# A gated linear attention kernel with two projections after it: tiles of q, k and exponentials laid out by chunk, guard reductions held behind layer two's slots

## Chip, core and metric

The kernel runs on one core of one Trainium2 chip. The metric is the device time of one execution in microseconds, the median of several runs. Engines are named as the profile names them: PE (TensorE), DVE (VectorE), ACT (ScalarE), POOL (GpSimd) and SP (SyncE, here only a queue that issues DMAs).

## Reference

4 batches of 8 heads, 768 steps, head size 48. A complex decay per step and channel, its magnitude clipped to 0.999, acts on a 48 x 48 state; then come two dense layers over 3072 tokens.

```python
mag = np.sqrt(a_re * a_re + a_im * a_im)
scale = np.minimum(mag, 0.999) / (mag + 1e-06)
a_re_n, a_im_n = (a_re * scale, a_im * scale)
for t in range(S):
    new_re = ar * S_re - ai * S_im
    new_im = ar * S_im + ai * S_re
    S_re, S_im = (new_re + kv, new_im)          # kv = outer(k[t], v[t])
    y[:, :, t] = np.einsum('bhd,bhde->bhe', q[:, :, t], S_re)
# layer one (384 -> 2048 -> 384), layer two the same with another gate
h = x @ w_in; g = h * np.clip(h + 3.0, 0.0, 6.0) / 6.0;         x = g @ w_out
h = x @ w_in; g = h * (1.0 / (1.0 + np.exp(-1.702 * h)));       out = g @ w_out
```

## The kernel before

Only the function `chunked_path` runs its work here; `general_path` behind it is taken when a flag says that the inputs left the range that the fast path assumes. The flag comes from guards: small reductions on DVE whose results `check_range` gathers.

**Preparation** (`prep_ops`). The 3072 tokens form 12 blocks of 256 tokens, each of two chunks of 128. For one block, 384 feature rows lie as three groups j of 128 partitions. ACT and DVE turn the decay into running products E and rotations cos and sin, and multiply q and k by them. The tiles `qk` and `E` (named `pE` in the profile) have the shape [128, q or k, (j, chunk), 129]: 128 steps, and one column more for the last decay. Block 0 is prepared chunk by chunk, the others whole.

**Repacking** (`repack`, L478 to L487). Attention wants heads on 96 partitions, so DMAs copy from `E` and `qk` into the tile `QK` ([96, 16, 129]; 48 partitions from `E`, 48 from `qk`). A chunk takes 12 DMAs: per source two of 48 partitions and 6 x 129 words, and four small ones for the rows that the three groups have left over. They alternate between the queues of SP and POOL, in block 0 between SP, POOL and ACT. Two buffers of `QK` exist (tag QK); the raw weights of layer two and the guards' loads use the same two.

**Attention** (`att_ops`). Per chunk PE makes scores (`sc`, L518), DVE masks them (`p`, L522), PE turns k (`kt`) and adds up the outputs (`yps`) and the state (`ud`). `slot(q, h)` says which of the 16 slots of `QK` holds a head's q or k.

**Layers.** One slot is an input projection (`h`, L635, nine matmuls), a gate in four steps on ACT and DVE (`gate1` to `gate4`; `gh` L655, `gl` L660) and an output projection (`o`, L673) that follows two slots later. A layer has 16 slots for each block of 512 tokens, six such blocks; at the end of a block ACT copies three accumulators out (`y`, L677) before PE can start the next block's output projections.

**Order.** For the first 82 slots of layer one, the text `PLAN` fixes the order on DVE, ACT and PE by hand. SP's and POOL's queues, and everything after the plan, are ordered by the compiler's planner, which places an instruction where its own estimate of time finds it ready.

**Guards.** After the plan `wdecode` loads, checks (`check_w`, L374) and decodes layer two's weights, 16 loads of 768 KB. In layer two `recheck_w` loads layer one's 16 weight tiles again and checks them, `recheck_a` loads four tiles of `a`, then `check_range` follows; the program hands them to the planner behind the slots `end[last + FT + 8 + i * 3]`; `last` is the first slot of layer one's last block, so `last + FT` is layer two's slot 0, and the guards stand at its slots 8, 11, 14 and so on to 68.

Of the kernel before, what the change touches and what calls it, by code (L numbers as in the profile page):

```python
# [9 lines left out]
F32 = mybir.dt.float32  # L10
# [4 lines left out]
AF = mybir.ActivationFunctionType  # L15
ALU = mybir.AluOpType
# [241 lines left out]
def chunked_path(ctx: ExitStack, tc, flag, a_t, qk_t, v_t, w1i, w1o, w2i, w2o, out):  # L258
# [34 lines left out]
    def stat_col(k, n=1):  # L293
        n_used[k] += n
        return stat[k][:, n_used[k] - n:n_used[k]]
# [44 lines left out]
    raw, w32, marks, wparts = {}, {}, {}, {}  # L340

    def load_w(m, kind, j):
        src = ((w1i, w1o), (w2i, w2o))[m][kind]
        t = at2.tile([P, 768, 2], U32, tag="QK", name="ws")
        nc.sync.dma_start(out=t.rearrange("p n w -> p (n w)"), in_=src[j].bitcast(U32))
        return t

    def recheck_w(i):
        check_w(load_w(0, i % 2, i // 2))

    def recheck_a(p):
        t = at2.tile([P, 768], F32, tag="QK", name="as")
        nc.sync.dma_start(out=t, in_=a_t[p, :, 0:3 * TB])
        V.tensor_reduce(out=stat_col("re"), in_=t, axis=mybir.AxisListType.X, op=ALU.min)

    def load_first(i):
        kind, j = i % 2, i // 2
# [13 lines left out]
        split_lo(V, 0, i % 2, i // 2, w32.pop(i))  # L371

    def check_w(t):
        V.tensor_reduce(out=stat_col("w"), in_=t.bitcast(F32)[:, :, 1], axis=mybir.AxisListType.X, op=ALU.min, apply_absolute_value=True)  # L374

    def split_hi(m, kind, j, x):
        w = wp.tile([P, 2, 768], F32R, tag=f"w{'io'[kind]}{j}", name=f"w{'io'[kind]}{j}")
# [14 lines left out]
    def load_in(b, parts="aq", c=None):  # L392
        if "a" in parts:
            if (b, "a") not in ins:
                ins[b, "a"] = prep.tile([P, 2, 3, TB], F32, tag="a", name="a")
            o, n = (0, TB) if c is None else (c * CH, CH)
            nc.sync.dma_start(out=ins[b, "a"].rearrange("p q j t -> p (q j) t")[:, :, o:o + n],
                              in_=a_t[b].rearrange("p (q j t) -> p (q j) t", q=2, j=3)[:, :, o:o + n])
        if "q" in parts:
            if (b, "qk") not in ins:  # L400
                ins[b, "qk"] = prep.tile([P, 2, 6, CE], F32, tag="qk", name="qk")
            qk = ins[b, "qk"]
            if c is None:
                nc.sync.dma_start(out=qk[:, :, :, 0:CH], in_=qk_t[b].rearrange("p (q c t) -> p q c t", q=2, t=CH))
            else:
                nc.sync.dma_start(out=qk.rearrange("p q (j c) t -> p (q j) c t", c=2)[:, :, c, 0:CH],
                                  in_=qk_t[b].rearrange("p (q j t) -> p (q j) t", q=2, t=TB)[:, :, c * CH:c * CH + CH])

    v_c = {}

# [4 lines left out]
    def prep_ops(b, c0, nch):  # L415
# [1 line left out]
        ts = c0 * CH  # L417
        ops = {}
        op = ops.__setitem__
        both = lambda t: t.rearrange("p q (j c) t -> p q j c t", c=2)[:, :, :, c0, 0:CH] if nch == 1 else t[:, :, :, 0:CH]  # L420
        bothc = lambda t: t.rearrange("p (j t) -> p j t", t=CH).unsqueeze(1).to_broadcast([P, 2, 3 * nch, CH])

        def tmp(nm):
            if (b, nm) not in ins:
                ins[b, nm] = prep.tile([P, 2, 6, CE] if nm == "E" else [P, 3 * TB], F32, tag=nm if nm == "E" else "p" + nm, name="p" + nm)
# [7 lines left out]
        sel = lambda t, q: t[:, q].rearrange("p (j c) t -> p j c t", c=2)[:, :, c0:c0 + nch, 0:CH]  # L433
        selc = lambda t: t.rearrange("p (j c t) -> p j c t", j=3, c=nch)
        col = lambda t, i: t.rearrange("p q (j c) t -> p q j c t", c=2)[:, :, :, c0:c0 + nch, i]
# [29 lines left out]
        op("turns", lambda: V.tensor_scalar(out=pB(), in0=pB(), scalar1=MAGIC, scalar2=None, op0=ALU.subtract))  # L465
        op("frac", lambda: V.scalar_tensor_tensor(out=pA(), in0=pA(), scalar=2.0 / TURN, in1=pB(), op0=ALU.mult, op1=ALU.subtract))
        op("keep", lambda: V.tensor_scalar(out=carry, in0=r3(pA())[:, :, n - 1:n], scalar1=0.5 * TURN, scalar2=0.0, op0=ALU.mult, op1=ALU.add))
        op("sin", lambda: tact(pC(), pA(), AF.Sin, scale=TURN))
        op("abs", lambda: act(pB(), pA(), AF.Abs))
        op("cos", lambda: tact(pB(), pB(), AF.Sin, scale=-TURN, bias=bhp))  # L470
        op("qkE", lambda: V.tensor_tensor(out=both(qk()), in0=both(qk()), in1=both(E()), op=ALU.mult))
        for d, t in (("qk", qk), ("E", E)):
            op("last" + d, lambda t=t: tact(col(t(), CH), selc(pC())[:, :, :, CH - 1].unsqueeze(1).to_broadcast([P, 2, 3, nch]), AF.Exp, scale=0.5))
        op("qkcos", lambda: V.tensor_tensor(out=both(E()), in0=both(qk()), in1=bothc(pB()), op=ALU.mult))  # L474
        op("qksin", lambda: V.tensor_tensor(out=both(qk()), in0=both(qk()), in1=bothc(pC()), op=ALU.mult))

        def repack(c, y, queues):
            if 2 * b + c not in qk_c:  # L478
                qk_c[2 * b + c] = at2.tile([96, 16, CE], F32, tag="QK", name="QK")
            t = qk_c[2 * b + c][48 * y:48 * y + 48]  # L480
            z = ins[b, "E" if y == 0 else "qk"].rearrange("p q (j c) t -> p q j c t", c=2)[:, :, :, c, :]
            parts = [(t[:, 6 * g:6 * g + 6, :], z[48 * g:48 * g + 48].rearrange("p q j t -> p (q j) t")) for g in range(2)]
            parts += [(t[d0:d0 + nr, 2 * h:2 * h + 2, :], z[r0:r0 + nr, :, j, :]) for r0, nr, j, h, d0 in ((96, 32, 0, 6, 0), (96, 16, 1, 6, 32), (112, 16, 1, 7, 0), (96, 32, 2, 7, 16))]
            for i, (dst, src) in enumerate(parts):
                e = (nc.sync, nc.gpsimd, nc.scalar)[i % (3 if b == 0 else 2)]
                if e in queues:
                    e.dma_start(out=dst, in_=src)  # L487
# [8 lines left out]
    xs = {}  # L496

    def slot(q, h):
        return (h % 2) * 6 + q * 3 + h // 2 if h < 6 else 2 * h + q

    def att_ops(c):
        b = c // 2
# [68 lines left out]

        def um():
            u = ud4() if first else u4
            g = qk_c[c][:, 0:12, CH:CE].rearrange("p (r q i) c -> p q i r c", r=2, q=2)[:, 1].to_broadcast([96, 3, 2, D])
# [41 lines left out]
    ht, gt, ops_ = {}, {}, {}  # L616
    slots = []
    for m in range(2):
        for b in range(NT // TK):
# [37 lines left out]

    def gate4(s):
        lo = gp.tile([P, s[3], s[5]], F32R, tag="gl", name="gl")
        V.tensor_tensor(out=lo, in0=gt[s][0], in1=gt[s][1], op=ALU.subtract)  # L660
        gt[s].append(lo)

    def outproj(s):
# [47 lines left out]
    def wload(n=1):  # L711
        for _ in range(n):
            if n_loaded[0] < len(wseq):
                raw[n_loaded[0]] = load_w(*wseq[n_loaded[0]])
                n_loaded[0] += 1

    def wdecode(x):
        i = n_decoded[0]
        check_w(raw[i])
        decode_weight(V, raw.pop(i), x)  # L720
        w32[i] = x
        n_decoded[0] += 1
        wload()
# [55 lines left out]
    with tc.manual_schedule(engines={mybir.EngineType.DVE, mybir.EngineType.Activation, mybir.EngineType.PE}):  # L779
        for token in PLAN.split():  # L780
            planned(token)

    end = {i: [] for i in range(len(slots))}
    last = slots.index((0, NT // TK - 1, 0, 1, 0, TK))
    wload(2)
    for k in range(2 * NPR):
        at = N_PLAN + k * (FT + 8) // (2 * NPR)
        end[at].append(lambda k=k: wdecode(spare(k)))
        end[max(at, last + k // 2 * 2 + 2 + k % 2 * LAG)].append(wsplit)
    at, n = last + 2 * FT, len(slots) - last - 3 * FT  # L790
    late = [lambda i=i: recheck_w(i) for i in range(2 * NPR)] + [lambda p=p: recheck_a(p) for p in range(LATE)] + [check_range]
    for i, f in enumerate(late):
        end[last + FT + 8 + i * 3].append(f)
    for c in range(NT // CH):
        end[slots.index((1, c * CH // TK, 0, 1, 0, TK)) - FT + 4 + 2 * (c % (TK // CH))].append(lambda c=c: load_x2(c))
    for i in range(N_PLAN, len(slots)):
# [59 lines left out]
```

## Time and profile before

| | us |
|---|---|
| median of three runs | 1019.45 (1017.28 to 1020.99) |
| the profiled execution | 1014.48 |
| its span, first to last instruction | 1012.8 |
| PE busy in it | 953.2 |
| DVE busy | 643.1 |
| ACT busy | 519.7 |

The profile is one execution. Times in it run from the start of the span. A line such as L518 is the line of the kernel. In a wait, the name behind the arrow is what ended last before the waiting instruction could start. PEclk is the granted share of TensorE's clock: 1.00 is the level of 2.4 GHz, 0.50 that of 1.2 GHz.

### The profile page before, as it was taken

How to read it: one execution, taken by the hardware profiler on the slowest of the kernel's cores; microseconds unless marked ns; L12 is line 12 of the kernel's file. 1: busy time of each engine (PE TensorE's matmuls, PEld its weight loads, DVE VectorE, ACT ScalarE, POOL GpSimd, SP SyncE). 2: the span in 40 equal slices, each digit the busy share in tenths (PEclk: the TensorE clock that was granted, in tenths of full speed). 3: DMA queues.
4: the chain of work that ended last, by engine and by line, in shares of the span. 5: the costliest groups of instructions: out<-in, count | busy, mean ns of one | idle time of the engine just before them, and what ended most of it. 6: DMA issues, size and time to landing. Idle time of an engine off the chain costs nothing.

```text
span 1012.8 us, 14367 instructions
## 1 busy us (share of the span) xinstructions
PE 953.2 (94%) x5378; PEld 802.7 (79%) x5378; DVE 643.1 (63%) x919; ACT 519.7 (51%) x862; POOL 111.8 (11%) x218
## 2 busy tenths in 40 slices
PE   1479999999999999999999999989999999999997
PEld 1378988898788888887788888768888888888885
DVE  6789998885866777577549998573343433433332
ACT  5767677675765786566426554233243333433322
POOL 2110212213303123030310000000000000000000
PEclk9779999999999999999999999999999999999999
DMA  8873425354535254233325447670020010100001
GB/s 307 246 234 79 127 63 111 97 122 111 117 90 139 64 126 117 56 96 94 71 83 191 138 151 224 238 233 21 1 63 1 24 40 1 47 1 1 32 1 34
DMA packets 82524, 101.04 MB, mean 100 GB/s; under 512 B 9104, under 2 KB 71824, under 8 KB 82448
## 3 DMA queue, kind: packets, MB, share of 16 engines
q1 hardware_dynamic: 73872, 88.44, 29.4%
q0 software_dynamic: 7936, 11.36, 5.0%
q8 instruction: 44, 0.72, 0.3%
q10 hardware_dynamic: 640, 0.26, 0.1%
q14 instruction: 32, 0.26, 0.1%
HBM read 67.63 MB, written 9.44 MB: 76 GB/s over the span
## 4 chain that ended last, share of the span: by engine, by line
PE 70%; DVE 15%; DMA 9%; ACT 3%; issue 2%; SPq 0%; DVEq 0%; ACTq 0%
PE o L673 29%; PE h L635 29%; PE sc L518 4%; DMA ws<-in_w1i 4%; PE ud L564 2%; PE yps L538 2%; DVE stat_w L374 2%; DVE gl L660 2%; PE yps L540 1%; DVE tt L648 1%; DMA xf<-x2d 1%; DMA QK<-qk 1%; DVE sp L127 1%; PE kt L527 1%; DVE sp L125 1%
## 5 line engine op out<-in xcount | busy, mean ns | idle before, releaser
L673 PE MATMUL o<-gh,wo 128*128 128x512 f32 (+1 forms) x1248 | 364.7, 376 | 4.1 <-ACT y L677 3.1
L635 PE MATMUL h<-xh,wi 128*128 128x512 f32 (+1 forms) x1248 | 364.9, 377 | 0.5 <-DVE wi L387 0.5
L673 PEld LDWEIGHTS o<-gh,wo 128*128 128x128 f32 x1248 | 225.9, 189 | 47.7 <-ACT y L677 4.3
L635 PEld LDWEIGHTS h<-xh,wi 128*128 128x128 f32 x1248 | 228.4, 190 | 42.2 <-issue 1.3
L635 PE MATMUL h<-xl,wi 128*128 128x512 f32 (+1 forms) x624 | 234.0, 375 | 1.1 <-DVE xl L607 1.1
L673 PE MATMUL o<-gl,wo 128*128 128x512 f32 (+1 forms) x624 | 234.2, 375 | 0.5 <-DVE gl L660 0.5
L655 ACT ACTIVATE gh<-tt 128x512 fp32r<-128x512 f32 x192 | 120.7, 630 | 131.4 <-DVE tt L650 92.1
L660 DVE TENSOR_TENSOR gl<-tt,gh 128x512 fp32r<-128x512 f32 x192 | 132.0, 689 | 70.0 <-ACT gh L655 69.4
L650 DVE TENSOR_TENSOR tt<-tt,h 128x512 f32<-128x512 f32 x96 | 65.9, 686 | 145.7 <-ACT tt L642 145.7
L673 PEld LDWEIGHTS o<-gl,wo 128*128 128x128 f32 x624 | 117.7, 189 | 23.9 <-DVE gl L660 3.1
L635 PEld LDWEIGHTS h<-xl,wi 128*128 128x128 f32 x624 | 118.4, 190 | 22.4 <-DVE xl L607 1.4
L642 ACT ACTIVATE tt<-h 128x512 f32<-128x512 f32 x96 | 57.1, 595 | 151.3 <-PE h L635 150.6
L640 ACT ACTIVATE tt<-h,b 128x512 f32<-128x512 f32 x96 | 65.4, 685 | 79.8 <-PE h L635 67.1
L648 DVE SCALAR_TENSOR_TENSOR tt<-tt,h 128x512 f32<-128x512 f32 x96 | 65.2, 684 | 39.9 <-ACT tt L640 39.6
L518 PE MATMUL sc<-QK 96*128 96x128 f32 x384 | 52.5, 284 | 14.8 <-DMA QK<-qk 11.0
L518 PEld LDWEIGHTS sc<-QK 96*128 96x128 f32 x384 | 49.0, 197 | 17.7 <-DMA QK<-qk 11.1
L487 POOL DMA_DIRECT2D QK<-pE x70 | 39.3, 567 | 176.4 <-DVE pE L474 119.7
L552 POOL DMA_DIRECT2D xf<-ysb x60 | 30.7, 518 | 235.6 <-ACT ysb L544 220.2
L522 DVE TENSOR_TENSOR p<-sc,causal 128x512 f32<-128x512 f32 x48 | 32.7, 687 | 26.8 <-PE sc L518 21.9
L538 PE MATMUL yps<-p,v 128*64 128x128 f32 (+1 forms) x384 | 40.9, 295 | 3.4 <-DVE p L522 2.5
L374 DVE TENSOR_REDUCE stat_w<-ws 128x1 f32<-128x768 f32 x32 | 30.4, 951 | 20.1 <-DMA ws<-in_w1i 10.2
L487 POOL DMA_DIRECT2D QK<-qk x70 | 38.9, 562 | 4.8 <-DMA QK<-pE 1.4
(111 smaller groups left out, 874.2 us busy)
## 6 DMA issues: line engine op xcount, KB each, us to landing
qk<-in_qk_t SPq DMA_DIRECT2D x12, 768.0 KB, 5.6
a<-in_a_t SPq DMA_DIRECT2D x11, 768.0 KB, 4.4
wr<-in_w1i SPq DMA_DIRECT2D x8, 768.0 KB, 9.0
wr<-in_w1o SPq DMA_DIRECT2D x8, 768.0 KB, 7.1
ws<-in_w2i SPq DMA_DIRECT2D x8, 768.0 KB, 4.4
ws<-in_w2o SPq DMA_DIRECT2D x8, 768.0 KB, 4.6
ws<-in_w1i SPq DMA_DIRECT2D x8, 768.0 KB, 5.8
ws<-in_w1o SPq DMA_DIRECT2D x8, 768.0 KB, 5.3
```

The source lines that it names most:

```text
L374: V.tensor_reduce(out=stat_col("w"), in_=t.bitcast(F32)[:, :, 1], axis=mybir.AxisListType.X, op=ALU.min, apply_absolute_value=True)
L487: e.dma_start(out=dst, in_=src)
L518: T.matmul(out=sc[:, i, :], lhsT=kv_(4 * g + i), rhs=qv(4 * g + i), start=True, stop=True)
L538: T.matmul(out=yps[r0:r1, h // 2, :], lhsT=v_c[c][:, e], rhs=s_["p", g][:, i, :], start=True, stop=first)
L635: T.matmul(out=h[:, i, :], lhsT=w[:, k, :], rhs=x[:, k, :], start=(k == 0 and q == 0), stop=(k == 2 and q == 2))
L640: A.activation(out=t, in_=ht[s], func=AF.Relu, bias=b3)
L642: A.activation(out=t, in_=ht[s], func=AF.Sigmoid, scale=1.702)
L648: V.scalar_tensor_tensor(out=t, in0=t, scalar=6.0, in1=ht[s], op0=ALU.min, op1=ALU.mult)
L650: V.tensor_tensor(out=t, in0=t, in1=ht[s], op=ALU.mult)
L655: A.activation(out=hi, in_=gt[s][0], func=AF.Copy)
L660: V.tensor_tensor(out=lo, in0=gt[s][0], in1=gt[s][1], op=ALU.subtract)
L673: T.matmul(out=acc[:, o:o + n], lhsT=w[:, e * P:e * P + P], rhs=g[:, i, :], start=(f == o == q == 0), stop=(f == FT - 1 and q == 2), skip_ ...
```

## The change

Three things are altered. First, `qk` and `E` become [128, chunk, j, q or k, 129]: all that one chunk needs on a partition is one run of 6 x 129 words (3,096 bytes), and a left-over row's q and k are one run of 2 x 129 words (1,032 bytes). Before, every run was 129 words (516 bytes). The slots of `QK` follow in the order (j, q or k). The operations on these tiles keep their element counts and read and write through other access patterns. The load of `qk` from memory, one DMA per block, becomes four, by chunk and by q or k. Second, the guards: `check_w` leaves `wdecode`, and `recheck_w` covers both layers' weights, so 32 loads stand in layer two instead of 16; every guard is held behind the latest `gate4` before it; the places are `end[last + FT + 16 + i * 3 // 2]`, one guard every one and a half slots from slot 16 of layer two's 96 to slot 69, with `check_range` at slot 70. Third, the lists of what follows each slot are built ahead of the plan; the tokens of the plan and their order are the same.

```diff
     def recheck_w(i):
-        check_w(load_w(0, i % 2, i // 2))
+        check_w(load_w(i // (2 * NPR), i % 2, i // 2 % NPR))
...
-        V.tensor_reduce(out=stat_col("re"), in_=t, axis=mybir.AxisListType.X, op=ALU.min)
+        r = V.tensor_reduce(out=stat_col("re"), in_=t, axis=mybir.AxisListType.X, op=ALU.min)
+        after(r, tail[0])
...
     def check_w(t):
-        V.tensor_reduce(out=stat_col("w"), in_=t.bitcast(F32)[:, :, 1], axis=mybir.AxisListType.X, op=ALU.min, apply_absolute_value=True)
+        r = V.tensor_reduce(out=stat_col("w"), in_=t.bitcast(F32)[:, :, 1], axis=mybir.AxisListType.X, op=ALU.min, apply_absolute_value=True)
+        after(r, tail[0])
...
-            if (b, "qk") not in ins:
-                ins[b, "qk"] = prep.tile([P, 2, 6, CE], F32, tag="qk", name="qk")
-            qk = ins[b, "qk"]
-            if c is None:
-                nc.sync.dma_start(out=qk[:, :, :, 0:CH], in_=qk_t[b].rearrange("p (q c t) -> p q c t", q=2, t=CH))
...
+            qk = ins[b, "qk"] = prep.tile([P, 2, 3, 2, CE], F32, tag="qk", name="qk")
+            src = qk_t[b].rearrange("p (q j c t) -> p q j c t", q=2, j=3, c=2)
+            for c in range(2):
+                for q in range(2):
+                    nc.sync.dma_start(out=qk[:, c, :, q, 0:CH], in_=src[:, q, :, c, :])
...
-        both = lambda t: t.rearrange("p q (j c) t -> p q j c t", c=2)[:, :, :, c0, 0:CH] if nch == 1 else t[:, :, :, 0:CH]
-        bothc = lambda t: t.rearrange("p (j t) -> p j t", t=CH).unsqueeze(1).to_broadcast([P, 2, 3 * nch, CH])
+        both = lambda t: t[:, c0:c0 + nch, :, :, 0:CH].rearrange("p c j q t -> p (c j) q t")
+        bothc = lambda t: t.rearrange("p (x t) -> p x t", t=CH).unsqueeze(2).to_broadcast([P, 3 * nch, 2, CH])
...
-        op("sin", lambda: tact(pC(), pA(), AF.Sin, scale=TURN))
-        op("abs", lambda: act(pB(), pA(), AF.Abs))
+        op("sin", lambda: tact(byc(pC()), selc(pA()), AF.Sin, scale=TURN))
+        op("abs", lambda: act(byc(pB()), selc(pA()), AF.Abs))
...
-            z = ins[b, "E" if y == 0 else "qk"].rearrange("p q (j c) t -> p q j c t", c=2)[:, :, :, c, :]
-            parts = [(t[:, 6 * g:6 * g + 6, :], z[48 * g:48 * g + 48].rearrange("p q j t -> p (q j) t")) for g in range(2)]
-            parts += [(t[d0:d0 + nr, 2 * h:2 * h + 2, :], z[r0:r0 + nr, :, j, :]) for r0, nr, j, h, d0 in ((96, 32, 0, 6, 0), (96, 16, 1, 6, 32), (112, 16, 1, 7, 0), (96, 32, 2, 7, 16))]
+            z = ins[b, "E" if y == 0 else "qk"][:, c]
+            parts = [(t[:, 6 * g:6 * g + 6, :], z[48 * g:48 * g + 48].rearrange("p j q t -> p (j q) t")) for g in range(2)]
+            parts += [(t[d0:d0 + nr, 2 * h:2 * h + 2, :], z[r0:r0 + nr, j, :, :]) for r0, nr, j, h, d0 in ((96, 32, 0, 6, 0), (96, 16, 1, 6, 32), (112, 16, 1, 7, 0), (96, 32, 2, 7, 16))]
...
-        return (h % 2) * 6 + q * 3 + h // 2 if h < 6 else 2 * h + q
+        return (h % 2) * 6 + (h // 2) * 2 + q if h < 6 else 2 * h + q
...
-        V.tensor_tensor(out=lo, in0=gt[s][0], in1=gt[s][1], op=ALU.subtract)
+        tail[:] = [V.tensor_tensor(out=lo, in0=gt[s][0], in1=gt[s][1], op=ALU.subtract)]
...
     def wdecode(x):
         i = n_decoded[0]
-        check_w(raw[i])
...
-    late = [lambda i=i: recheck_w(i) for i in range(2 * NPR)] + [lambda p=p: recheck_a(p) for p in range(LATE)] + [check_range]
+    late = [lambda i=i: recheck_w(i) for i in range(4 * NPR)] + [lambda p=p: recheck_a(p) for p in range(LATE)] + [check_range]
     for i, f in enumerate(late):
-        end[last + FT + 8 + i * 3].append(f)
+        end[last + FT + 16 + i * 3 // 2].append(f)
```

`after` adds an edge that only orders two instructions of one engine's queue; it makes no engine wait for another.

## Rows read from the trace of the kernel before

**Rows 1.** the page: the span and the engines' busy time with its share.
```profile
span 1012.8 us, 14367 instructions
...
PE 953.2 (94%) x5378; PEld 802.7 (79%) x5378; DVE 643.1 (63%) x919; ACT 519.7 (51%) x862; POOL 111.8 (11%) x218
```

**Rows 2.** windows: from:to, length, busy PE PEld DVE ACT POOL, PEclk, DMA share, GB/s.
```profile
25.00:50.00 25.00, 11.14 (x90) 9.41 (x89) 20.09 (x32) 18.00 (x33) 3.04 (x6) 0.78 0.82 245
...
50.00:75.00 25.00, 19.86 (x134) 17.95 (x134) 22.34 (x28) 16.06 (x25) 3.70 (x7) 0.74 0.70 236
...
200.00:300.00 100.00, 96.65 (x686) 84.46 (x685) 73.61 (x103) 68.88 (x117) 26.60 (x50) 1.00 0.49 115
```

**Rows 3.** waits of PE, whole run: sum in us, times, longest.
```profile
PE warm L747 <- ACT pB L331: 21.5, 1, 21.5
...
PE sc L518 <- DMA QK<-qk: 11.0, 1, 11.0
...
PE sc L518 <- issue: 1.8, 2, 1.1
...
PE kt L527 <- DMA QK<-qk: 0.8, 1, 0.8
```

**Rows 4.** chain of work that ended last, 20 to 50 us: start, length, what.
```profile
24.89 4.21 DMA QK<-pE
...
41.40 6.82 DMA QK<-qk
```

**Rows 5.** DVE in order of time, 30 to 53 us: start, length, last idle.
```profile
30.47 0.69 DVE L522 TENSOR_TENSOR p<-sc,causal 128x512 f32<-128x512 f32 x1 [0.43 <-PE sc L518]
...
50.38 0.69 DVE L522 TENSOR_TENSOR p<-sc,causal 128x512 f32<-128x512 f32 x1 [2.57 <-PE sc L518]
...
52.08 0.69 DVE L522 TENSOR_TENSOR p<-sc,causal 128x512 f32<-128x512 f32 x1 [1.01 <-PE sc L518]
```

**Rows 6.** DMA issues of the page: count, KB each, median us to landing.
```profile
QK<-pE SPq DMA_DIRECT2D x24, 145.1 KB, 3.9
...
QK<-qk SPq DMA_DIRECT2D x24, 145.1 KB, 4.4
...
xf<-ysb SPq DMA_DIRECT2D x20, 72.0 KB, 2.7
```

**Rows 7.** windows, columns as in group 2: repacking alone, then one weight load.
```profile
74.00:82.00 8.00, 8.00 (x71) 8.00 (x70) 6.86 (x11) 4.04 (x7) 3.70 (x7) 1.00 0.78 146
...
592.00:598.00 6.00, 6.00 (x28) 4.99 (x27) 6.00 (x10) 2.68 (x4) 0.00 (x0) 1.00 0.42 131
```

**Rows 8.** line 404, its issue on SP's queue and who waited for it.
```profile
L404 SPq DMA_DIRECT2D qk<-in_qk_t x12: 546/602/610, 4.0 to 462.9; - x12
...
  DVE qk L471: 1.4, 1
```

**Rows 9.** DVE lines from 627 to 684 us, and landings of tile ws there.
```profile
L374 DVE TENSOR_REDUCE stat_w<-ws 128x1 f32<-128x768 f32 x15 | 14.3, 952 | 16.2 <-DMA ws<-in_w1i 10.2 <-DMA ws<-in_w1o 6.0
...
DMA to landing us min/median/max: 4.1/5.8/6.2
```

**Rows 10.** waits of PE, 600 to 700 us, and the window that follows them.
```profile
PE o L673 <- ACT y L677: 3.1, 2, 2.7
...
PE o L673 <- ACT gh L655: 0.9, 1, 0.9
...
684.30:687.70 3.40, 3.40 (x10) 2.46 (x9) 1.38 (x2) 1.53 (x3) 0.00 (x0) 0.50 0.48 154
```

**Rows 11.** DVE at the last guard and two steady slots; one full window.
```profile
680.89 0.95 DVE L354 TENSOR_REDUCE stat_re<-as 128x1 f32<-128x768 f32 x1 [0.39 <-DMA as<-in_a_t]
...
702.11 0.69 DVE L650 TENSOR_TENSOR tt<-tt,h 128x512 f32<-128x512 f32 x1 [2.00 <-ACT tt L642]
...
706.18 0.69 DVE L650 TENSOR_TENSOR tt<-tt,h 128x512 f32<-128x512 f32 x1 [2.00 <-ACT tt L642]
...
632.00:660.00 28.00, 27.83 (x121) 22.26 (x120) 14.46 (x19) 6.51 (x12) 0.00 (x0) 1.00 0.67 228
```

More of the change, by code (lines that the diff above doesn't have):

```diff
@@ L339, in chunked_path @@
     wi, wo = {}, {}
-    raw, w32, marks, wparts = {}, {}, {}, {}
+    raw, w32, wparts = {}, {}, {}
     def load_w(m, kind, j):
@@ L399, in load_in @@
         if "q" in parts:
-            if (b, "qk") not in ins:
-                ins[b, "qk"] = prep.tile([P, 2, 6, CE], F32, tag="qk", name="qk")
-            qk = ins[b, "qk"]
-            if c is None:
-                nc.sync.dma_start(out=qk[:, :, :, 0:CH], in_=qk_t[b].rearrange("p (q c t) -> p q c t", q=2, t=CH))
-            else:
-                nc.sync.dma_start(out=qk.rearrange("p q (j c) t -> p (q j) c t", c=2)[:, :, c, 0:CH],
-                                  in_=qk_t[b].rearrange("p (q j t) -> p (q j) t", q=2, t=TB)[:, :, c * CH:c * CH + CH])
+            qk = ins[b, "qk"] = prep.tile([P, 2, 3, 2, CE], F32, tag="qk", name="qk")
[3 more added lines that the diff above has]
+                    nc.sync.dma_start(out=qk[:, c, :, q, 0:CH], in_=src[:, q, :, c, :])
     v_c = {}
@@ L419, in prep_ops @@
         op = ops.__setitem__
-        both = lambda t: t.rearrange("p q (j c) t -> p q j c t", c=2)[:, :, :, c0, 0:CH] if nch == 1 else t[:, :, :, 0:CH]
-        bothc = lambda t: t.rearrange("p (j t) -> p j t", t=CH).unsqueeze(1).to_broadcast([P, 2, 3 * nch, CH])
+        both = lambda t: t[:, c0:c0 + nch, :, :, 0:CH].rearrange("p c j q t -> p (c j) q t")
+        bothc = lambda t: t.rearrange("p (x t) -> p x t", t=CH).unsqueeze(2).to_broadcast([P, 3 * nch, 2, CH])
         def tmp(nm):
             if (b, nm) not in ins:
-                ins[b, nm] = prep.tile([P, 2, 6, CE] if nm == "E" else [P, 3 * TB], F32, tag=nm if nm == "E" else "p" + nm, name="p" + nm)
+                ins[b, nm] = prep.tile([P, 2, 3, 2, CE] if nm == "E" else [P, 3 * TB], F32, tag=nm if nm == "E" else "p" + nm, name="p" + nm)
             return ins[b, nm] if nm == "E" else ins[b, nm][:, 3 * ts:3 * ts + 3 * n]
@@ L432, in prep_ops @@
         r3 = lambda t: t.rearrange("p (j t) -> p j t", j=3)
-        sel = lambda t, q: t[:, q].rearrange("p (j c) t -> p j c t", c=2)[:, :, c0:c0 + nch, 0:CH]
-        selc = lambda t: t.rearrange("p (j c t) -> p j c t", j=3, c=nch)
-        col = lambda t, i: t.rearrange("p q (j c) t -> p q j c t", c=2)[:, :, :, c0:c0 + nch, i]
+        sel = lambda t, q: t[:, c0:c0 + nch, :, q, 0:CH]
+        selc = lambda t: t.rearrange("p (j c t) -> p c j t", j=3, c=nch)
+        byc = lambda t: t.rearrange("p (c j t) -> p c j t", j=3, c=nch)
         mp = mask_p if nch == 2 else mask_l
@@ L472, in prep_ops @@
         for d, t in (("qk", qk), ("E", E)):
-            op("last" + d, lambda t=t: tact(col(t(), CH), selc(pC())[:, :, :, CH - 1].unsqueeze(1).to_broadcast([P, 2, 3, nch]), AF.Exp, scale=0.5))
+            op("last" + d, lambda t=t: tact(t()[:, c0:c0 + nch, :, :, CH], selc(pC())[:, :, :, CH - 1].unsqueeze(3).to_broadcast([P, nch, 3, 2]), AF.Exp, scale=0.5))
         op("qkcos", lambda: V.tensor_tensor(out=both(E()), in0=both(qk()), in1=bothc(pB()), op=ALU.mult))
@@ L573, in um @@
             u = ud4() if first else u4
-            g = qk_c[c][:, 0:12, CH:CE].rearrange("p (r q i) c -> p q i r c", r=2, q=2)[:, 1].to_broadcast([96, 3, 2, D])
+            g = qk_c[c][:, 0:12, CH:CE].rearrange("p (r i q) c -> p q i r c", r=2, q=2)[:, 1].to_broadcast([96, 3, 2, D])
             V.tensor_tensor(out=u4[:, 0:3], in0=u[:, 0:3], in1=g, op=ALU.mult)
@@ L613, in load_x2 @@
         split_lx(1, c, xf)
-    ht, gt, ops_ = {}, {}, {}
+    ht, gt, ops_, tail = {}, {}, {}, []
     slots = []
@@ L777, in planned @@
             memo[at][k]()
-    with tc.manual_schedule(engines={mybir.EngineType.DVE, mybir.EngineType.Activation, mybir.EngineType.PE}):
-        for token in PLAN.split():
-            planned(token)
     end = {i: [] for i in range(len(slots))}
     last = slots.index((0, NT // TK - 1, 0, 1, 0, TK))
-    wload(2)
     for k in range(2 * NPR):
@@ L790, in chunked_path @@
     at, n = last + 2 * FT, len(slots) - last - 3 * FT
-    late = [lambda i=i: recheck_w(i) for i in range(2 * NPR)] + [lambda p=p: recheck_a(p) for p in range(LATE)] + [check_range]
+    late = [lambda i=i: recheck_w(i) for i in range(4 * NPR)] + [lambda p=p: recheck_a(p) for p in range(LATE)] + [check_range]
     for i, f in enumerate(late):
-        end[last + FT + 8 + i * 3].append(f)
+        end[last + FT + 16 + i * 3 // 2].append(f)
     for c in range(NT // CH):
         end[slots.index((1, c * CH // TK, 0, 1, 0, TK)) - FT + 4 + 2 * (c % (TK // CH))].append(lambda c=c: load_x2(c))
+    with tc.manual_schedule(engines={mybir.EngineType.DVE, mybir.EngineType.Activation, mybir.EngineType.PE}):
+        for token in PLAN.split():
+            planned(token)
+    wload(2)
     for i in range(N_PLAN, len(slots)):
```

## The prediction

> **What bounds the kernel now.** I read the page first, then windows, then what PE waited for, and last the two stretches where it waits. PE is busy 953.2 us of a span of 1012.8 us [rows 1], so nothing that leaves PE's work alone can save more than some 60 us, and 21.5 us of those are the wait ahead of PE's first matmul, before any repacking [rows 3]. In the waits of PE over the whole run three kinds can be touched here. One is repacked tiles: 11.0 us once for the second chunk, 0.8 us once for a transpose, and 1.8 us in two waits that the view puts down to "issue" but that end when a tile of a burst lands [rows 3]. The second is in layer two behind the guards: 3.1 and 0.9 us of waits, and right after them 3.4 us in which the granted clock is 0.50, the 1.2 GHz level, where it had been 1.00 [rows 10]. The third is the low clock of the start, 0.78 and 0.74 over 25 to 75 us [rows 2]. Elsewhere PE has work all the time, so a gain there shows only if it shortens one of these.
>
> **Repacking, the start.** A chunk's copies move 2 x 128 rows of 6 x 129 words, 0.79 MB. The change leaves the bytes, the 12 DMAs, their queues and their order; it divides the runs by six (516 to 3,096 bytes) or by two. What is a long run worth? In a window that holds only repacking, the 16 DMA engines are busy 0.78 of the time and move 146 GB/s: 146 / (16 x 0.78) = 11.7 GB/s for each busy engine. In a window with one weight load, 6,144 bytes in a run, it is 131 / (16 x 0.42) = 19.5 [rows 7]. A chunk at these rates takes 0.79 MB / (16 x 11.7) = 4.2 us or 2.5 us, so up to 1.7 us less. The other bound comes from landings: 3.9 and 4.4 us for the large pieces, against 2.7 us for a copy of the same 48 partitions in runs of 1,536 bytes but half the bytes [rows 6]: 1.2 to 1.7 us less. I take 1.6 us a chunk; the ends are 0 (a load queued ahead decides the landing) and 1.7.
>
> Who is paid? At the start DVE is busy 20.09 and 22.34 us of two stretches of 25 [rows 2] and sets the pace; PE's idle time costs nothing of itself. The two landings on the chain are 4.21 us (first chunk) and 6.82 us (second) [rows 4]. For the first, DVE waited only 0.43 us at its mask [rows 5], so 1.6 us earlier saves 0.4. For the second, DVE waited 2.57 us and then 1.01 us [rows 5]; the second wait is PE's own work at the low clock and stays. All of the 1.6 us fits into the 2.57. Sum for the start: 2.0 us, between 0 and 3.0 (0.43 + 2.57). What is late next is DVE itself.
>
> The Trainium skill speaks against this part: its page "DMA: Bandwidth & Descriptors", section Specifications, gives 512 bytes as the least transfer for line rate, and its section on small descriptors says that "SBUF↔SBUF transfers don't suffer this penalty". By that page 516 bytes are enough and both repacking terms would be 0. The trace does not agree, with 11.7 against 19.5 GB/s, though the second figure is for a load from memory.
>
> **Repacking, later.** The waits of 0.8 and 1.8 us [rows 3] are three waits of 1.1 us at most each; pieces that land 1.6 us earlier remove up to 2.6 us. What is late next is the projection or mask beside them, so I take 2.0, between 0 and 2.6.
>
> **The loads of qk.** One DMA becomes four, 12 times: 36 more issues on SP's queue of 0.60 us each [rows 8]. The last quarter is issued 3 x 0.60 = 1.8 us later; behind it on SP stand the next loads of `a` and `v` and the stores of layer one. The load may start only when the block before is repacked, which is now 1.6 us earlier, so it lands about 0.2 us later. Only one block waited for it, 1.4 us [rows 8], and DVE had over 26 us to spare in the 100 us around that place [rows 2]. I take 0; the bounds are -1 and +3.6 us (two blocks late by 1.8 us, if that cover is gone).
>
> **Access patterns.** `qkE`, `qkcos`, `qksin`, `sin` and `abs` keep their element counts; runs of 128 words stay runs of 128 words. I take 0. No row shows the new patterns; if DVE or ACT took 1% longer on them it would be lost in their idle time after the start. Bounds 0 and +1.
>
> **Guards.** Before, 15 weight guards ran between 627 and 684 us at 952 ns each, and DVE stood idle 16.2 us ahead of them for their loads [rows 9]; each next load had to wait until a guard freed its buffer. DVE takes its queue in order, so the gate's steps stood behind each of those waits. The delay reached PE at the end of layer two's first block: the last guard waits 0.39 us and holds DVE 0.95 us [rows 11], ACT's copy of the accumulators stands behind it, and PE waits 3.1 us; with the 0.9 us wait and the clock (3.4 us at half, so 1.7 us) this is 5.7 us [rows 10].
>
> After, 36 guards stand one in 1.5 slots. A slot takes 706.18 - 702.11 = 4.07 us and leaves DVE idle 2.00 us ahead of `tt` alone [rows 11]; a guard takes 0.95 of that, behind `gl`, and delays nothing. Its load can go once the guard two before it is done, 3 slots or 12.2 us ahead, against landings of 6.2 us at most [rows 9]. The loads ask for (32 x 0.786 + 4 x 0.393 MB) / (54 x 4.07 us) = 122 GB/s; PE was busy 27.83 of 28 us while 228 GB/s moved [rows 11]. On SP the loads are queued with the stores of y and the loads of x; a load that waits for its buffer holds these for at most the 6.1 us between two guards. The 16 reductions that leave the decoding free 15 us of DVE where PE had no wait to speak of: 0. The last guard runs some 26 slots before the end, so the flag is early. I take all 5.7 us; the ends are 0 and 5.7.
>
> **Sum.** 2.0 + 2.0 + 5.7 = 9.7 us. The profiled execution took 1014.48 us (span 1012.8 and 1.7 around it), so it would give 1004.8. The median of the runs shown is 1019.45, 5.0 above that execution; I carry the difference over: 1009.7.
>
> **Rivals.**
> - The runs' length buys nothing, since fixed costs and loads queued ahead decide when a tile lands. For it: the second chunk's 6.82 us [rows 4] is far above the 4.4 us median [rows 6], so something other than its runs delayed it. Against it: the rates of [rows 7]. Only the guards pay: 1019.45 - 5.7 = 1013.7. This is also what the page named above would give. 0.18.
> - The guards' loss moves instead of going: DVE still waits for loads, at a later block's end. Only repacking pays: 1019.45 - 4.0 = 1015.5. Against it: 12.2 us of lead. 0.12.
> - The quarter loads of qk come late at two blocks (+3.6), PE loses its clock once more (+1.7) and repacking's later gain is gone: 2.0 + 5.7 - 5.3 = 2.4, so 1017.0. 0.08.
> - Slower: a guard's load is held on SP behind stores, and DVE waits for it at the end of a block. Three ends of blocks (slots 32, 48 and 64) lie in the new stretch, where before there was one. Each could cost what that one cost, 3.1 + 1.7 = 4.8 us: 14.4, less 5.7 removed and 4.0 of repacking: +4.7, so 1024.2. It decides once a load lands more than 12.2 us after the guard that freed its buffer. Loads landed in 6.2 at most. 0.06.
>
> **How the numbers follow.** The forecast has 0.56 and 1009.7. The best case is 3.0 + 2.6 + 5.7 and 1.7 for the low clock at the start, 13.0, so 1006.4; the runs shown lie up to 2.2 us below their median, so the low end is 1004. The high end takes in the first two rivals and most of the third: 1018. Outside lie the slower rival and a few hundredths more. About 0.3% (3 us) can be told from no change: faster means under 1016.4, slower over 1022.5. Faster: nearly all of the forecast and of the first rival, 0.7 of the second, 0.4 of the third, 0.54 + 0.15 + 0.08 + 0.03 = 0.80. Slower 0.06, the rest 0.14.
>
> **What would show it.** After the change, the chain's second landing should read near 5.2 us and DVE's wait at that mask near 1 us; the large pieces should land in under 3 us; PE should show no wait and no window at 0.50 near layer two's first block's end; the guards should show no idle time ahead of them for DMA. A second landing still near 6.8 us makes the first rival right; waits of PE for `y` around slots 32, 48 or 64 the last. Quarter loads for which `qk` at L471 waits more than 1.4 us would break the step on SP's queue.

## The result, and the profile after

The changed kernel takes 1001.78 us (median of 4, 1000.25 to 1004.47) beside 1019.04 us of the kernel before (1017.28 to 1020.99): ratio 0.9833, interval 0.9805 to 0.9861, so 17.3 us less. The forecast was 1009.7 and the range 1004 to 1018: the direction was right, the gain nearly twice the one forecast, and the time lies below the range. The profiled execution after took 1002.03 us (span 1000.3), against 1014.48 before: 12.45 us less. Where single executions were plainly disturbed (one of 5408 us) the medians below leave them out.

The page after, answering to [rows 1]:

```profile
PE 948.5 (95%) x5378; PEld 802.7 (80%) x5378; DVE 645.6 (65%) x919; ACT 520.3 (52%) x862; POOL 104.9 (10%) x218
```

PE does the same 5378 matmuls in a span 12.5 us shorter. Its view of DMA issues, answering to [rows 6] (the loads of qk and the repacking's large pieces; count, KB each, median us to landing):

```profile
qk<-in_qk_t SPq DMA_DIRECT2D x48, 192.0 KB, 3.5
QK<-pE POOLq DMA_DIRECT2D x24, 145.1 KB, 3.7
QK<-qk SPq DMA_DIRECT2D x24, 145.1 KB, 3.5
...
QK<-pE SPq DMA_DIRECT2D x24, 145.1 KB, 3.6
```

The waits of PE over the whole run, answering to [rows 3]:

```profile
PE warm L745 <- ACT pB L331: 21.5, 1, 21.5
PE sc L517 <- DMA QK<-qk: 9.7, 1, 9.7
...
PE sc L517 <- issue: 0.6, 1, 0.6
```

The wait of `kt` is gone, "issue" fell from 1.8 to 0.6, and the second chunk's wait from 11.0 to 9.7. In layer two PE has no wait at all. The chain of work that ended last, which answers to [rows 4] for the first chunk only:

```profile
24.80 3.80 DMA QK<-pE
34.71 9.53 DMA wr<-in_w1i
44.26 2.67 DMA QK<-qk
```

SP's issues of the second chunk's copies from `qk` (two of them; the second is the one of 44.26), and PE's first score of that chunk:

```profile
41.12 3.65 SPq L486 DMA_DIRECT2D QK<-qk  x2
46.53 2.69 PE L517 MATMUL sc<-QK 96*128 96x128 f32 x11 [9.74 <-DMA QK<-qk]
```

DVE in order of time, answering to [rows 5]:

```profile
29.97 0.69 DVE L521 TENSOR_TENSOR p<-sc,causal 128x512 f32<-128x512 f32 x1 [0.52 <-PE sc L517]
...
48.61 0.69 DVE L521 TENSOR_TENSOR p<-sc,causal 128x512 f32<-128x512 f32 x1 [2.14 <-PE sc L517]
```

And a window, answering to [rows 2]:

```profile
50.00:75.00 25.00, 19.48 (x135) 17.75 (x134) 22.43 (x29) 15.63 (x25) 5.45 (x11) 0.74 0.71 236
```

The second chunk's last piece waits at its issue: SP held it 2.4 us until a weight load (`wr`) had landed, and the piece then took 2.67 us. From it the chain runs on over SP's queue. PE's first score waited for another piece: the large one issued at 41.12 us, which landed at 46.39, so 5.27 us after its issue, against 6.82 before ([rows 4]). The second chunk's first mask comes at 48.61 us instead of 50.38, 1.77 us earlier, though DVE's own wait there only fell from 2.57 to 2.14. The granted clock over 50 to 75 us is 0.74 as before.

The guards in the view of DVE's lines, with the idle time ahead of them in the last column, answering to [rows 9]:

```profile
L375 DVE TENSOR_REDUCE stat_w<-ws 128x1 f32<-128x768 f32 x32 | 30.3, 947 | 0.0
```

The same window of layer two, of the kernel before and then of the changed one (columns as in [rows 2]):

```profile
650.00:700.00 50.00, 45.81 (x185) 34.64 (x184) 28.47 (x44) 15.67 (x29) 0.00 (x0) 0.97 0.51 173
```

```profile
650.00:700.00 50.00, 50.00 (x222) 41.42 (x221) 24.39 (x35) 18.24 (x31) 0.00 (x0) 1.00 0.37 126
```

Read PE's counts in brackets (x185 and x222), not the busy time. At full rate 50 us hold 222 matmuls, 0.225 us each. The kernel before issued 185 in the same time: 37 fewer, 8.3 us lost, while its busy time shows only 50 - 45.81 = 4.2 us without work. The rest is the half clock (1.5) and stalls too short for the view of waits, since the ends of matmuls are modelled and lie over them.

The starts show where: from 652 us on, output projections of the kernel before start 0.2 to 1.1 us late, well ahead of the long wait at the block's end.

Both kernels issue the same matmuls in the same order (only the two small ones of `check_range` come two slots later after the change), so the starts of the n-th matmul in the two traces can be subtracted. How much later the kernel before gets in each stretch:

```
stretch (us)   before minus after   of it at the half clock in one of them
0 to 75              0.99               -0.52
75 to 200            1.83                1.58
200 to 300          -0.22               -1.52
300 to 520           1.48                0.00
520 to 740           8.62                1.49
740 to the end       0.00                0.00
```

So 4.1 us of this pair lie ahead of 520 us, with the repacking, and 8.6 in the guards' stretch.

### The profile page after: what moved, and what is told of

Read it like the earlier page. It is cut to its first block, busy times and chain, and to the rows that moved or that the text cites. A ratio compares the mean times of both kernels' runs of the same rounds, so it can differ in the third digit from the quotient of the medians.

```text
span 1000.3 us, 14460 instructions
## 1 busy us (share of the span) xinstructions
PE 948.5 (95%) x5378; PEld 802.7 (80%) x5378; DVE 645.6 (65%) x919; ACT 520.3 (52%) x862; POOL 104.9 (10%) x218
## 4 chain that ended last, share of the span: by engine, by line
PE 88%; DVE 4%; DMA 3%; ACT 2%; issue 1%; SPq 1%; ACTq 0%; DVEq 0%
PE h L634 38%; PE o L672 38%; PE sc L517 4%; PE yps L537 2%; PE ud L563 2%; PE yps L539 2%; DMA wr<-in_w1i 1%; PE kt L526 1%; DMA xf<-ysb 1%; DVE pE L473 0%; DMA x2d<-y 0%; DMA a<-in_a_t 0%; DVE gl L659 0%; DMA QK<-pE 0%; ACT pB L331 0%
## 5 line engine op out<-in xcount | busy, mean ns | idle before, releaser
L517 PE MATMUL sc<-QK 96*128 96x128 f32 x384 | 52.3, 284 | 11.9 <-DMA QK<-qk 9.7
L517 PEld LDWEIGHTS sc<-QK 96*128 96x128 f32 x384 | 48.9, 197 | 14.5 <-issue 13.2
L486 POOL DMA_DIRECT2D QK<-pE x70 | 35.7, 516 | 175.5 <-DVE pE L473 117.0
L486 POOL DMA_DIRECT2D QK<-qk x70 | 35.3, 510 | 6.5 <-DMA QK<-pE 2.9
L563 PE MATMUL ud<-v,ks 128*96 128x48 f32 x320 | 31.9, 254 | 4.2 <-ACT ks L531 4.2
```

Of the source, the lines that this page charges most:

```text
L517: T.matmul(out=sc[:, i, :], lhsT=kv_(4 * g + i), rhs=qv(4 * g + i), start=True, stop=True)
L563: T.matmul(out=ud[:, h, :], lhsT=s_["ks"][:, h, :], rhs=v_c[c][:, h * D:h * D + D], start=True, stop=True)
```

## Experiments

Two theories stood at first. A: the guards cost the kernel before more than its profile shows (12 to 14 us), the layout brings 3 to 5. B: the guards cost 8 to 9 us and the layout was counted too low (8 to 9).

**The kernel before, once more** (no edit).

> The kernel before, unchanged, taken again with a profile. The profiled execution of before took 1014.5 us, the others 1017.3 to 1021.0. Theory A (the guards in layer two pay differently from execution to execution): this profile lies at 1017 to 1021 us, and the stretch of 600 to 700 us holds more waits of PE than the 4.2 us and the 3.4 us at half clock seen before, or another stretch at half clock. Theory B (the first profile is typical, and the changed kernel gains in places no profile of before shows): the same waits again, within 1 us. Ratio to before 1.000 +- 0.002.

1017.39 us in 12 executions (ratio 1.0019, 0.999 to 1.0048). Another 35 executions beside it lay between 1008.03 and 1022.37, median 1016.82. Its new profile, an execution of 1022.49 us, has 180 matmuls in 650 to 700 us, 9.5 us lost. The 1014.48 us of the first profile are on the quick side: 12 of the 35 executions were quicker. Counted from the first matmul on, the matmuls of this slower execution get later by 7.4 us against the first profile: 2.5 up to 75 us, 3.8 between 75 and 520 us, and 1.1 in the guards' stretch.

**The guards' part alone.** The changed kernel with the old layout, loads and `slot`.

> The kernel before with the guards' change alone: out of the decoding, both layers' weights in layer two, held behind the latest gate step, spread over slots 16 to 69. Theory A: guards give most of the 17 us, 12 to 14 us faster than before (ratio 0.987); no wait of PE and no half clock between 600 and 700 us. Theory B: 8 to 9 us faster (ratio 0.9915), the rest belongs to the layout.

1008.29 us (1006.06 to 1011.56 in 12), 8.5 below the median before. PE has no wait between 502 and 1000 us.

**The edges alone.** The guards keep their old number and places:

```diff
+        r = V.tensor_reduce(out=stat_col("re"), ...)
+        after(r, tail[0])            # and the same in check_w
-        V.tensor_tensor(out=lo, ...)
+        tail[:] = [V.tensor_tensor(out=lo, ...)]
```

> The kernel before with the edges alone: each guard held behind the last subtraction of its slot, with the guards' old number, places and spacing and the old layout. If the edges do the work, this gives what the whole guard change gave alone: ratio 0.9936, about 6.5 us, with no TensorE stalls in 650 to 700 us and a small spread of the executions. If place and spacing do it, the stalls of 2 us each stay and the ratio is 1.000.

1008.31 us (1006.55 to 1009.11), ratio 0.9913 (0.989 to 0.9937): all that the guards' part gave. The window in which the kernel before lost 37 matmuls is full:

```profile
650.00:700.00 50.00, 50.00 (x222) 41.39 (x221) 22.23 (x33) 18.66 (x32) 0.00 (x0) 1.00 0.28 95
```

**The changed kernel without the edges.**

```diff
-        after(r, tail[0])            # in recheck_a and in check_w
```

> The changed kernel without the edges that hold each guard behind the last subtraction of its slot (the calls of after(r, tail[0])); the guards keep their new number, place and spacing. If the edges do the work, guards run up in front of the slots' subtractions again: TensorE shows stalls in 650 to 700 us, and the time is 4 to 8 us above the changed kernel. If the place and the spacing do it (one guard every one or two slots, later in layer two), there are no stalls and the time is within 1.5 us of the changed kernel.

1015.35 us, ratio 0.9981 (0.9956 to 1.0006): the gain is all but gone. The 32 weight guards ran in one burst again (602.7 to 705.5 us) instead of 667 to 855, though the program hands them over at the new, wider places. This kernel's guards in the view of DVE's lines, and its windows:

```profile
L374 DVE TENSOR_REDUCE stat_w<-ws 128x1 f32<-128x768 f32 x32 | 30.5, 953 | 30.2 <-DMA ws<-in_w1i 8.7 <-DMA ws<-in_w1o 8.2 <-DMA ws<-in_w2o 7.2
```

```profile
600.00:650.00 50.00, 49.03 (x215) 39.98 (x214) 30.94 (x42) 17.97 (x31) 0.00 (x0) 1.00 0.77 258
650.00:700.00 50.00, 41.62 (x165) 30.96 (x164) 29.34 (x41) 14.44 (x26) 0.00 (x0) 0.97 0.81 266
```

7 and 57 matmuls are missing: 14.4 us. DVE stood idle 30.2 us ahead of guards whose loads had not landed. So the edge does the work, not the places.

**The kernel before without layer two's guards** (the re-check of layer one's weights and of the late inputs is left out).

```diff
     for i, f in enumerate(late):
-        end[last + FT + 8 + i * 3].append(f)
+        if f is check_range:
+            end[last + FT + 8 + i * 3].append(f)
```

> The kernel before without its re-check of layer one's weights and of the late inputs in layer two (that part of the guard is left out). If the edges took all that these guards cost, this is the time of the edges alone, 1008.3 within 1.5 us (ratio 0.991). If guards that are held still cost something (their loads beside the matmuls, DVE behind the slots), this is 1 to 4 us faster than the edges alone. The executions should agree as closely as with the edges, within 4 us, if the guards are what spreads the kernel before.

1009.57 us, ratio 0.9931 (0.9908 to 0.9954): not below the edges alone. Once held, guards cost nothing that can be measured. The executions spread over 4.8 us, a little more than the 4 us expected.

**The layout alone.** The changed kernel with the guards' old count, places and no edges.

> The changed kernel with its guards as they were before: the layout by chunk, long runs and the qk load in four pieces alone. Theory A: 3 to 5 us faster than before (ratio 0.996), as the two profiles show up to 600 us (4.2 us). Theory B: 8 to 9 us faster (ratio 0.9915).

1010.81 us (1007.7 to 1015.13). Its profile loses 44 matmuls in 650 to 700 us, 9.9 us; without them it would be at 1001, the changed kernel's time. So the layout gives 6.0 us at the median, between the two theories, and the guards' 8.5 to 8.9 are as B had them.

**The changed kernel beside the kernel before, twice more** (no edit).

> The changed kernel itself once more, beside the kernel before, in many more executions of both. If the parts simply add, its ratio is the product of the two parts alone, 0.9936 (guards alone) times 0.9962 (layout alone) = 0.990, some 10 us: then the first comparison, 0.983 on four executions each, was high by chance of the executions. If the two parts help each other (one part hides what the other gives back), the ratio stays near 0.983, some 17 us. The times of single executions say something too: the kernel before spread over 14 us in 35 executions, the guards alone over 5.5 us in 12; if the guards are what spreads the kernel before, the changed kernel spreads over no more than 5 us.

1000.55 us beside 1017.26: ratio 0.9844 (0.9814 to 0.9875). That is nearer to the parts helping each other than to the product of their ratios, 0.990. By medians the parts alone make 8.5 + 6.0 = 14.5 us, against 16.7 here for both at once; whether the rest is the spread of the kernel before or help between the parts isn't settled.

> The changed kernel beside the run before it on the same chip. It gave 1001.8 and 1000.6 us on two occasions; 1000.5 to 1002 is expected of every theory, with a ratio of 0.983 to 0.985.

1001.70 us beside 1017.84: ratio 0.9872 (0.9829 to 0.9915). All executions of the changed kernel but the one of 5408 us, 13, lie between 1000.06 and 1004.47, median 1001.5.

**Loads of qk by quarters, in the kernel before.**

```diff
+            for k in (0, 1) if c is None else (c,):
+                for q in range(2):
+                    nc.sync.dma_start(out=dst[:, q, :, k, 0:CH], in_=src[:, q, :, k, :])
```

> The kernel before, with only its load of q and k split into quarters (four transfers a block, two for a half block), in the old layout: nothing else moves. Short runs in the changed kernel's order gave 0.9974 where guards alone gave 0.9936, so something of the change besides the guards and the run length costs 3 to 4 us. If that is the split, this run shows a ratio of 1.003 to 1.004 and SP's small pieces or the loads behind them issued later; if the split is free, as the prediction's term of 0 has it, 1.000, and the 3 to 4 us lie with the access patterns or with chance.

1018.93 us, ratio 1.0011 (0.9993 to 1.0029): the split is free, as the prediction had it. The longest wait for a quarter was the same 1.4 us at `qk` L471 as before.

**Run length, nothing else moved.** In the changed kernel the two groups of heads take alternate rows of `QK`, so each run written is 516 bytes, while the runs read stay long; tiles, addresses, loads and order stay. First for the large pieces alone, then for the small ones too.

```diff
-            parts = [(t[:, 6 * g:6 * g + 6, :], ...
+            parts = [(t[:, g:12:2, :], ...
-            parts += [(t[d0:d0 + nr, 2 * h:2 * h + 2, :], ...      # second kernel
+            parts += [(t[d0:d0 + nr, h + 6:h + 9:2, :], ...        # second kernel
```

> The changed kernel with the large repacking pieces' runs broken on the receiving side: the two groups of heads take alternate rows of the repacked tile, so each run written is 516 bytes long again, while tiles, addresses, loads and the order of all steps are those of the changed kernel (the small pieces keep their runs of two rows). If the run length is worth what the pairs of equal matmul rate show, this is 4 to 5.5 us above the changed kernel, with large pieces landing in 4 us and more and a thousand layer-two matmuls in 226.58 us. If the layout pays by its order and its loads, not by its runs, it is within 1.5 us of the changed kernel.

1005.66 us, 4.0 above the changed kernel on the same chip.

> As the kernel with the large pieces' runs broken on the receiving side, and the small pieces' runs too (the two rows of a head now lie two rows apart): every run written is 516 bytes, as before the change, with sizes, addresses, loads and the order of steps of the changed kernel. If all of the layout's gain is run length, this is the guards' time alone, 1008.3 within 1.5 us. If the small pieces' runs count for nothing, it stays at 1005.7 within 1.2, and 2.6 us belong to the order by chunk and the loads.

1008.39 us (1006.71 to 1009.51): the time of the guards alone. So all that the layout brings, some 7 us, is run length: about 4 from the large pieces, 2 to 3 from the small ones; the order by chunk and the quarter loads bring nothing that can be measured. Its large pieces land in 3.8 to 4.2 us again, and PE's waits for them are back (this kernel's DMA issues, then its waits of PE):

```profile
QK<-pE POOLq DMA_DIRECT2D x24, 145.1 KB, 4.2
QK<-qk SPq DMA_DIRECT2D x24, 145.1 KB, 4.0
```

```profile
PE sc L517 <- issue: 2.0, 2, 1.3
...
PE kt L526 <- DMA QK<-qk: 0.8, 1, 0.8
```

Against the changed kernel's third profile, its matmuls get later by 0.5 us between the first of them and 75 us, and by 6.0 between 75 and 520 us. Of these 6.0 us, 3.5 show as idle time of PE, 1.5 are one stretch at half clock, and the rest are shorter stalls.

The trace's DMA packets show the price of a run as the prediction reckoned it, bytes over the busy time of an engine. Up to 520 us, packets of 516 bytes move at 11.9 GB/s in the kernel before and in this one; packets of 3,096 bytes move at 15.5 in the changed kernel. All repacking together goes from 12.9 to 15.8 GB/s, or from 3.85 to 3.14 us a chunk on 16 engines. Shortness may not be all of it: up to 100 us the loads of `qk` from memory, in runs of 512 bytes, move at 17.2 GB/s in the kernel before, and its packets of 516 bytes at 11.8. These loads are copies of another kind, and no run here repacked in runs of 512 bytes, so what makes 516 slow is open.

**Short runs by padding.** Rows of the tiles padded by one word, then by four.

```diff
-            qk = ins[b, "qk"] = prep.tile([P, 2, 3, 2, CE], ...)
+            qk = ins[b, "qk"] = prep.tile([P, 2, 3, 2, CE + 1], ...)   # E likewise; second kernel CE + 4
```

> The changed kernel with one more word behind each run in the tiles of q, k and exponentials, so that repacking reads runs of 516 bytes again; orders of all engines, slots, the qk load in four pieces and the guards stay. If the length of runs is what the layout pays with, this is 3 to 4 us slower than the changed kernel (1005 us, ratio to before 0.9865), the large pieces land in 3.9 to 4.4 us again and the first-chunk and second-chunk landings on the chain return to 4.2 and 6.8 us. If the run length buys nothing (the rival), it is within 1 us of the changed kernel (ratio 0.983).

1011.73 us: slower than the guards alone.

> Short runs again: rows of the tiles of q, k and exponentials padded by 16 bytes, so that each repacking run is 516 bytes as before the change, but now with all later tiles moved by 384 bytes, which keeps where they stand within 128. Order of all steps as in the changed kernel. If the run length is what the layout's part of the gain comes from, the time is that of the guards' part alone, 1008.3 within 1.5 us, with the repacking's large pieces landing in 4 us and more. If the address made most of the 11 us of the first kernel with short runs, the time is 1002 to 1004, and the run length is worth only 2 to 3 us.

1024.02 us, ratio 1.0061 (1.0039 to 1.0083): slower than the kernel before. Neither is explained by runs. In layer two, where nothing is repacked, a thousand matmuls took 228.76 and 233.17 us in them, 226.58 in the changed kernel. The padding had moved the tiles of x and of the gates by 64 and by 384 bytes (384 is 128 more than 256).

**Addresses alone.** The changed kernel, with an unused tile of 32, 64, 128, 256 or 512 bytes a partition ahead of the tiles of preparation, attention and layers, so that all of these move; constants and weights stay:

```diff
+    shift = prep.tile([P, n // 4], F32, tag="shift", name="shift")
```

> The changed kernel with an unused tile of 64 bytes a partition ahead of the attention's and the layers' tiles: their addresses move up by 64 bytes, to where the tiles of x and of the gates lay in the kernel with short runs; nothing else changes. In that kernel a thousand layer-two matmuls took 228.76 us, in the changed kernel and all others 226.58. If the address is the reason, this run shows 228.8 us for the same thousand, and with it a time 7 to 9 us above the changed kernel's (1008 to 1010). If the address is not the reason, 226.6 and the changed kernel's time, 1000.5 within 1.5 us, and short runs themselves cost 11 us.

> The same with 32 bytes. If what counts is where a tile stands within 64 bytes, this is the one that differs, and the thousand matmuls take more or less than 226.58 us; if what counts is where it stands within 128 bytes, it lies between the two known ones and may be either. If no address counts, 1000.5 us within 1.5. No theory gives a number below 226.58; a faster one would be a gain on the changed kernel.

> The changed kernel with all tiles from the attention on moved by 128 bytes (unused tile ahead of them). Moved by 32, 64 and 384 bytes a thousand layer-two matmuls took 233.2, 228.8 and 233.2 us instead of 226.6. If only where a tile stands within 128 bytes counted, 384 bytes would have changed nothing; so another distance counts, and this run may give either. If it gives 226.6 us for the thousand, the time is the changed kernel's within 1.5 us; at 228.8 about 1006, at 233.2 about 1019.

> The same by 512 bytes. If the distance that counts is a divisor of 512, the thousand matmuls take 226.6 us and the kernel 1000.5 within 1.5; if it is longer, the rate may be any of the three, and padded kernels can be compared only where their rates are equal.

> The changed kernel with all tiles from the attention on moved by 256 bytes. A thousand layer-two matmuls: 226.6 us if the distance that counts divides 256 (the time then 1000.5 to 1002), else 228 to 234 (1005 to 1020) as at 64, 128 and 384 bytes; below 226.6 would be a gain, for which nothing speaks so far.

```
moved by (bytes)      0        32        64       128       256      512
median (us)        1001.5    1019.47   1006.22   1019.5    1000.95  1001.21
```

The same 240 us of layer two in the changed kernel, moved by 64 and moved by 32 (columns: stretch, length, PE busy and count, PEclk, DMA share, GB/s):

```profile
740.00:980.00 240.00, 240.00 (x1061) 1.00 0.24 81
```

```profile
740.00:980.00 240.00, 240.00 (x1051) 1.00 0.25 82
```

```profile
740.00:980.00 240.00, 240.00 (x1031) 1.00 0.28 92
```

Busy time and clock are equal; 10 and 30 matmuls are missing. By the distances tried, what counts is where these tiles stand within 256 bytes. The unmoved tiles of x and of the gates start at the same remainder by 256 as the weights' tiles, so these runs don't tell a tile's own place from its distance to the weights. The kernel moved by 64 bytes is quicker than the 1008 to 1010 us expected of it. The pairs of padded kernels with equal matmul rate put the run length, broken on the reading side, at 1011.73 - 1006.22 = 5.5 and 1024.02 - 1019.47 = 4.6 us, somewhat below the 6.9 of the clean runs. No placement tried is faster than the changed kernel's own by more than 0.6 us, which is within its spread.

## Why the prediction was wrong

| term (us) | forecast | first two profiled executions | later runs |
|---|---|---|---|
| repacking, start | 2.0 | 1.0 | 0.5 (profiles, long against short runs) |
| repacking, later | 2.0 | 3.1 | 6.0 (the same profiles) |
| guards | 5.7 | 8.6 | 8.5 and 8.9 (medians) |
| sum | 9.7 | 12.7 | 15.0 to 15.4; 16.1 and 16.7 measured (medians) |

- **Guards: the mechanism right, the term mis-sized.** The step that failed is the sum of the waits of [rows 10] as the whole loss, with the delay reaching PE only at the block's end. The view gave 4.0 us, 5.7 with the clock; 37 missing matmuls say 8.3, clock included, and the stalls begin some 30 us ahead of the block's end. The row to read was the window's count, and it stood in the trace of before. In other executions and kernels without edges the same stretch lost 9.5 to 14.4 us.
- **Carrying the 5.0 us over to the median failed.** The prediction took the gap between the profiled execution and the median as something that stays. The spreads suggest that most of it is stalls that the change removes: the kernel before spreads over 14 us in 35 executions, the guards' part alone over 5.5 in 12, the edges alone over 2.6 in 6, the changed kernel over 4.4 in 13. The two profiles of the kernel before point the same way: 6.3 of the 7.4 us between them lie ahead of 520 us, with the repacking, and 1.1 with the guards. So the quick profiled execution understated both terms, the repacking more. With the forecast's 9.7 taken from the profiled execution, 1004.8, the miss would have been 3 us instead of 8.
- **Repacking: 4.1 for 4.0 in the first pair, in part by luck; too small at the median, and elsewhere than said.** At the start the landing that PE's score waits for fell from 6.82 to 5.27 us, 1.55 for 1.6 forecast, and the mask came 1.77 us earlier (DVE's wait there, which was to fall to near 1 us, was still 2.14). But 6.82 is the longest of all profiles: with 516-byte runs in the large pieces that landing takes 5.0 to 6.8 us (ten profiles, median 5.3), with long runs 4.6 to 5.8 (ten, median 4.9), so the runs are worth some 0.4 us there. And by 75 us 1.0 was left of the 1.77, with the low clock as long as before (23.9 us at 0.50 in both); the step that failed there ended its count at the mask. Later, the step that failed is the count of the three waits of [rows 3] as all that could be won: the clean pair shows 6.0 us there, with a stretch at half clock, waits for a mask and a gate, and stalls too short for the view.
- **The price of a chunk was too high, 1.6 us.** The 19.5 GB/s of [rows 7] belong to a load from memory; the changed kernel's 3,096-byte runs move at 15.5, and a chunk takes 0.7 us less. In the first pair a price twice too high was made up for by too few places where it is paid.
- **Large and small pieces.** The prediction's rate took a chunk as a whole, its landings only the large pieces. The runs give some 4 us to the four large pieces and 2 to 3 us to the eight small ones, whose runs only doubled.
- **The first rival fell, and with it the page beside it.** With 516-byte runs, all else equal, the kernel takes 1008.39 us, 6.9 more. The Trainium skill's page "DMA: Bandwidth & Descriptors", section Specifications, has 512 bytes as the least transfer for line rate; repacking in runs of 516 bytes does not reach the rate of longer runs here, 11.9 GB/s an engine against 15.5. What spoke for the rival was true: something besides the runs lengthens the second chunk's landing, which takes 5.27 us after the change too, far above the median of 3.5. A weight load was under way beside it in both kernels; that the load is the reason isn't shown. I had also written that large pieces would land in under 3 us; they took 3.5 to 3.7, only 0.3 to 0.9 less than before.
- **The other rivals didn't occur.** The guards' loss didn't move: no wait of PE between 500 and 900 us, at slots 32, 48 and 64 neither. Quarter loads: nobody waited for them after the change, and 0 was right. Access patterns at 0 were right within the noise: breaking the runs alone gave back all of the layout's gain.

## What to carry to other kernels

Where the ends of an engine's instructions are modelled, count its instructions per window against a full window: missing instructions give the loss, busy time only a part. Before carrying a profiled execution over to a median, ask whether their gap is made of what the change removes; if it is, the gain grows with the gap. An instruction that waits for a slow load in an in-order queue needs an edge that holds it, since a later place in the program did not keep the planner from moving it up.

## What the runs showed of the hardware

- A tile's address changed the matmul rate. With x and the gates (and the other tiles allotted behind them) moved by 32 or 128 bytes, a thousand 128x512 matmuls took 233.2 us, by 64 bytes 228.8, by 256 and 512 bytes 226.6 as unmoved, at granted clock 1.00. The Trainium skill's page "SBUF — State Buffer", section Operand start alignment, asks for a multiple of the element size and says that this is about legality, not speed; all of these addresses meet it, and here the time of the whole kernel changes by 18 us. Why is open; the weights' tiles weren't moved, and other distances weren't tried. Whoever pads a tile for an experiment should compare the matmul rate first.
- Every profile with 516-byte runs in the large pieces (ten) has at least one more stretch of 3.4 us at granted clock 0.50 after the start and outside the guards' stretch, at 1.5 us each; of the ten with long runs four do. The commonest one, near 255 us, comes right after a wait of PE of 2.0 us for a mask; the kernels without that stretch wait there just as long, so what decides it is open.
